# Row sums of an attention kernel taken for two head pairs at once, with a new order of work for the first eight steps

## The chip, the cores and the metric

The kernel runs on one core of a Trainium2 chip. The metric is device time in microseconds (us) of one execution of the whole kernel, lower is better. Below, the engines are called by the profile's names: PE (TensorE, matrix products; PEld is its weight loading), DVE (VectorE), ACT (ScalarE), POOL (GpSimd) and SP (SyncE, which issues DMAs).

## The reference

Attention with a soft cap on the scores, followed by a channel-mixing layer. Cut to what is computed:

```python
# B, H, S, D = 8, 12, 448, 64; float32
scores = cap * tanh(q @ k.T / sqrt(64) / cap)
attn = exp(scores - max) ; attn = attn / (sum(attn) + 1e-9)
x = (attn @ v)                      # to (8, 448, 768)
xk = mu_k * x + (1 - mu_k) * x_prev # x_prev: x shifted by one position
xr = mu_r * x + (1 - mu_r) * x_prev
k = relu(xk @ w_k)                  # 768 -> 1024
out = sigmoid(xr @ w_r) * ((k * k) @ w_v)
```

The three weights arrive as 64-bit numbers and are turned into float32 on the chip.

## The kernel before

**Pairs and steps.** The 96 heads are worked as 48 pairs of heads. Up to step 13 (`SW = 14`) the loop in `run` does one step `i` for each pair; later steps take two pairs at once and are the same in both kernels. A step is a list of words (`START_EVEN`, `START_ODD`), and `step` issues the operation of each word in the order of the list. Every engine takes its own instructions in the order in which they were issued, so the list is the program of all engines at once. A word works on a pair that hangs on the step: `S`, `L`, `tanh`, `exp`, `red` on pair `i`, `V` on pair `i - 1`, `sum_recip`, `norm`, `mix_old`, `mix_new`, `x_high`, `x_low`, `x_store`, `VL` on pair `i - 2`.

**What the words do.** The 448 keys are cut in three groups of 128 and a rest of 64; the rests of an even pair and of the odd pair behind it share one tile ("L", `p_left`).
- `S0 S1 S2` and `L` (PE, L275 and L285): scores of a key group, into one of two score tiles in PSUM. A tile can be written again once its `tanh` is done.
- `tanh`, `exp` (ACT, L291 and L301): 128 x 896 each, one `tanh` and one `exp` for each score tile.
- `V` (PE, L310): the six 64-column products with the values; `VL` (L319): the four products of the rest.
- `O` and `OL` (PE, L331 and L340): row sums, as products with a tile of ones (`self.one`, 1/32), for the pairs in `ONES` (0 to 5). The other pairs get their row sums from `red` (DVE, L356), `gather`, `recip`, `rec_store`, `rec_load`.
- `sum_recip` (DVE, L347 to L352): row sums from PSUM to reciprocals, spread over the partitions.
- `norm` (DVE, L407): values times reciprocal. `mix_old` (ACT, L417) then `mix_new` (DVE, L422) form `xk`; `mix_old` reads what `norm` wrote, `mix_new` reads what `mix_old` wrote. `x_high`, `x_low` (POOL, L127 and L137) split it for the key products.
- `K` (PE, L469): parts of `xk @ w_k`; the first falls into step 7 (`KFIRST = 28`).

**Weights beside it.** The 64-bit weights come in chunks. `weight_load` (SP, L501) loads one chunk, `more` loads extra ones in the steps named in `MORE`. `weight_abs` takes the absolute value of the high words of the loaded chunks, on DVE (L515) for the chunks in `DABS` and on ACT (L517) for the others. Each `f` then issues the next of five DVE operations (L537 to L545) on the chunks whose absolute value was issued, `weight_rest` those that are left; an `f` with no chunk does nothing. `weight_sum` (POOL, L554 and L127) and `weight_low` (DVE, L576) finish a chunk.

Of the kernel before, what the change touches and what calls it, by code (L numbers as in the profile page):

```python
# [9 lines left out]
F32 = mybir.dt.float32  # L10
F32R = mybir.dt.float32r
AF = mybir.ActivationFunctionType
ALU = mybir.AluOpType
# [3 lines left out]
B, H, S, D = 8, 12, 448, 64  # L17
# [6 lines left out]
NPAIR = B * NP  # L24
HN = DM // 2
P = 128
# [24 lines left out]
KO = (6, 4, 3, 2)  # L51
# [17 lines left out]
HALF = (slice(0, 64), slice(64, 128))  # L69
NB = 2 * S // 32  # L70
# [3 lines left out]

START_EVEN = """more weight_load gather load_qk load_v weight_store load_vl OL f sum_recip weight_low weight_rest S0 K S1 V
VL L relu tanh0 exp0 tanh1 k_store tanhL expL qk_high weight_sum f recip norm f red0 f S2 K exp1 relu mix_old
qk_low redL mix_new red1 x_high x_low k_store tanh2 K O K relu exp2 k_store f red2 weight_abs rec_store
x_store rec_load"""  # L80
START_ODD = """load_qk weight_load gather load_v sum_recip f f norm f f K S0 tanh0 exp0 mix_old relu k_store O K S1 S2 tanh2
# [8 lines left out]
LAST = """V.0 V.1 VL next gather l2 p0 recip d1 rec_store c0 rec_load l5 c1 k_store s0 c2 norm.0 norm.1 mix_old.0 mix_old.1  # L90
# [1 line left out]


def order(i):
    ops = LAST if i == NPAIR else UNIT if SW <= i <= NPAIR + 1 else START_ODD if i % 2 else START_EVEN
    if i == 8:
        ops = ops.replace("tanh2 K O K relu exp2", "K O K relu tanh2 exp2")
# [15 lines left out]
class Body:  # L113
# [189 lines left out]
    def values(self, i):  # L303

        nc, v = self.nc, self.rawv.pop(i)
        pv = self.ps_v.tile([P, 512], F32, name="pv")
        for g in range(3):
            ph = self.P32[i, g]
            for h, p in enumerate(HALF):
                nc.tensor.matmul(pv[p, 0:S], v[:, g, h, :], ph[:, h, :], start=(g == 0), stop=False)  # L310
        self.PV[i] = pv

    def values_left(self, i):


        v, ph = self.rawv.pop((i, "L")), self.P32[i, "L"]
        for p in range(2):
            for h, o in enumerate(HALF):
                self.nc.tensor.matmul(self.PV[i + p][o, 0:S], v[HALF[p], h, :], ph[HALF[p], h, :],  # L319
                                      start=False, stop=True)  # L320
# [13 lines left out]
    def ones_left(self, i):  # L334

        ph = self.P32[i, "L"]
        self.SUM[i + 1] = self.ps_k.tile([P, 512], F32, name="kps")
        for p in range(2):
            for h, o in enumerate(HALF):
                self.nc.tensor.matmul(self.SUM[i + p][o, 0:S], self.one[HALF[p]], ph[HALF[p], h, :],  # L340
                                      start=(p == 1), stop=(p == 0))

    def sum_recip(self, i):

        nc = self.nc
        t = self.up.tile([P, NB // 2], F32, name="se", bufs=1)
        nc.vector.tensor_reduce(out=t, in_=self.SUM.pop(i)[:, 0:S].rearrange("p (b k) -> p b k", k=32),  # L347
                                axis=mybir.AxisListType.X, op=ALU.add, apply_transpose=True)
        nc.vector.tensor_scalar(t, t, self.grd, None, op0=ALU.add)
# [444 lines left out]
    def step(self, i):  # L794

        even, unit = i % 2 == 0, SW <= i <= NPAIR + 1
        if unit and not even:
            return
        if self.maxima and even and i < NPAIR:
            self.row_maxima(i)  # L800
            self.row_maxima(i + 1)
        pair = dict(load_qk=i + 3, qk_high=i + 2, qk_low=i + 2, load_v=i, S=i, tanh=i, exp=i, red=i, load_vl=i, L=i)
        pair.update(dict.fromkeys("V gather recip rec_store rec_load".split(), i - 1))
        pair.update(O=i - 1, OL=i - 2)
        pair.update(dict.fromkeys("sum_recip norm mix_old mix_new x_high x_low x_store VL".split(), i - 2))
        name = dict(S="scores", V="values", VL="values_left", L="scores_left", O="ones", OL="ones_left")
        late = "gather recip rec_store rec_load red".split()
        first = "O OL sum_recip".split()
        two = "gather recip rec_store rec_load".split()
        nk = 0  # L810
        if unit:
            pair.update(VL=i - 2)
        seen = {}
        for op in order(i):
            g, j1 = (), 0
            if len(op) == 2 and op[0] in "lpdcs":
                self.tail_work(op)
                continue
            if "." in op:
                op, j1 = op[:-2], int(op[-1])  # L820
            if op[-1] in "012L" and op not in ("L", "VL", "OL"):
                op, g = op[:-1], (op[-1] if op[-1] == "L" else int(op[-1]),)
            if op in pair:
                j = pair[op] + j1
                if unit and op == "V":
                    j -= 1
                    if j < SW - 1:
                        continue
                if op in two:
                    if unit:  # L830
                        if j - 1 < NPAIR:
                            getattr(self, op + "_two")(j - 1)
                        continue
                    if j >= SW - 2:
                        continue
                if op == "load_qk" and i == 0 and Q2:
                    self.load_qk(2)
                if 0 <= j < NPAIR and op not in (late if j in ONES else first) and not (uncut(j) and op in ('qk_high', 'qk_low')):
                    getattr(self, name.get(op, op))(j, *g)
            elif op == "next":  # L840
                self.open_first()
# [216 lines left out]
```

## Time and profile before

| | |
|---|---|
| time, median of 3 runs | 896.61 us (896.44 to 896.88) |
| the profiled execution | 895.82 us, its span 894.0 us |
| PE busy | 881.2 us (99%) |
| DVE busy | 734.8 us (82%) |
| ACT busy | 623.1 us (70%) |
| POOL busy | 415.0 us (46%) |

The shares are means over the whole span. Times in the trace are counted from the start of the span. A timeline row gives the start, the time that the instructions took together, the engine, the line and the tiles; in square brackets stands how long the engine sat idle before and what ended that.

### The profile page before, as it was taken

To read this page: it belongs to the slowest core of one execution; us is meant where nothing else is said; L and a number is where in the kernel's file an instruction comes from. 1 tells how busy PE (TensorE), PEld (TensorE's weight loads), DVE (VectorE), ACT (ScalarE), POOL (GpSimd) and SP (SyncE) were. 2 spreads that over 40 slices of the span, in tenths; PEclk is the share of its full clock that TensorE was granted. 3 is DMA by queue.
4 is the path that set the end of the run, shared out by engine and by line. 5 is a ranking of instruction groups with operands and counts; after the bars stand their busy time and mean duration, and the time that the engine had idled before them with its cause. 6 is when DMAs were issued, how large, how long until landed. Compare 5 with 4: busy or idle time off the path is not lost.

```text
span 894.0 us, 14329 instructions
## 1 busy us (share of the span) xinstructions
PE 881.2 (99%) x5046; PEld 694.7 (78%) x5046; DVE 734.8 (82%) x1115; ACT 623.1 (70%) x962; POOL 415.0 (46%) x399
## 2 busy tenths in 40 slices
PE   7999999999999999999999999999999999999997
PEld 2335556767766677777676999999999999999996
DVE  5868996888987887897886789888888888888883
ACT  7898878888887787787876776655545555555451
POOL 2343354555566585676774003444345434443440
PEclk9999999999999999999999999999999999999999
DMA  7354655766656776677647963233233322332301
GB/s 261 118 167 144 207 185 163 227 193 192 193 184 193 210 224 214 201 216 243 200 148 247 330 237 95 76 110 118 79 114 110 118 87 85 119 110 83 119 28 49
DMA packets 97562, 142.97 MB, mean 160 GB/s; under 512 B 11592, under 2 KB 86984, under 8 KB 96840
## 3 DMA queue, kind: packets, MB, share of 16 engines
q1 hardware_dynamic: 89704, 129.56, 46.3%
q10 hardware_dynamic: 7776, 12.39, 3.7%
q8 instruction: 42, 0.69, 0.3%
q14 instruction: 40, 0.33, 0.1%
HBM read 94.18 MB, written 45.33 MB: 156 GB/s over the span
## 4 chain that ended last, share of the span: by engine, by line
PE 94%; ACT 3%; DVE 1%; DMA 1%; issue 0%; SPq 0%; DVEq 0%; ACTq 0%
PE kps L469 26%; PE ps2a L720 22%; PE pv L310 12%; PE ps2c L720 11%; PE s L275 11%; PE ps2b L720 5%; PE pv L319 2%; PE s L285 2%; PE kps L331 1%; ACT p L291 1%; ACT p L301 1%; DMA sq<-r 0%; DVE ro L708 0%; PE kps L340 0%; DMA w<-wk 0%
## 5 line engine op out<-in xcount | busy, mean ns | idle before, releaser
L291 ACT ACTIVATE p<-s,scl_t 128x896 f32<-128x896 f32 x144 | 139.4, 997 | 17.0 <-PE s L275 11.3
L301 ACT ACTIVATE p<-p,cap_t 128x896 f32<-128x896 f32 x144 | 145.2, 1036 | 1.9
L469 PE MATMUL kps<-xkh,wkl 128*128 128x448 f32 x384 | 143.5, 374 | 0.1
L469 PE MATMUL kps<-xkl,wkh 128*128 128x448 f32 x384 | 140.7, 366 | 0.0
L356 DVE TRANSPOSE_TENSOR_REDUCE r<-p 128x28 f32<-128x896 f32 x126 | 136.0, 1092 | 5.7 <-ACT p L301 5.4
L469 PE MATMUL kps<-xkh,wkh 128*128 128x448 f32 x384 | 140.3, 365 | 0.0
L310 PE MATMUL pv<-p,rv 128*64 128x448 f32 x576 | 115.1, 544 | 0.0
L469 PEld LDWEIGHTS kps<-xkh,wkl 128*128 128x128 f32 x384 | 72.1, 188 | 25.7 <-issue 12.3
L310 PEld LDWEIGHTS pv<-p,rv 128*64 128x64 f32 x576 | 38.6, 136 | 66.5 <-issue 57.4
L469 PEld LDWEIGHTS kps<-xkl,wkh 128*128 128x128 f32 x384 | 72.1, 188 | 8.0 <-issue 2.8
L469 PEld LDWEIGHTS kps<-xkh,wkh 128*128 128x128 f32 x384 | 72.1, 188 | 5.8
L708 DVE TENSOR_TENSOR ro<-t,ro 128x384 fp32r<-128x384 f32 x70 | 52.8, 756 | 23.2 <-ACT ro L131 23.2
L137 POOL TENSOR_TENSOR qkl<-rqk,qkh 128x832 fp32r<-128x832 f32 x34 | 67.6, 1988 | 2.7
L708 DVE TENSOR_TENSOR vo<-x,vo 128x512 fp32r<-128x512 f32 x63 | 56.3, 902 | 11.3 <-ACT vo L131 11.0
L407 DVE TENSOR_TENSOR x<-pv,r 128x448 f32<-128x448 f32 x48 | 28.1, 618 | 45.3 <-DMA r<-rec_d 43.6
L554 POOL TENSOR_TENSOR wsq<-wa,wsq 128x384 f32<-128x384 f32 x24 | 25.9, 1080 | 84.4 <-DVE wsq L545 84.4
L752 ACT ACTIVATE rs<-rs 128x384 f32<-128x384 f32 x28 | 14.7, 525 | 65.1 <-DVE rs L725 65.1
L131 ACT CAST ro<-t 128x384 fp32r<-128x384 f32 x70 | 34.3, 509 | 30.5 <-POOL t L137 30.2
L137 POOL TENSOR_TENSOR xkl<-xk,xkh 128x448 fp32r<-128x448 f32 x46 | 53.0, 1152 | 3.8
L672 DVE SCALAR_TENSOR_TENSOR t<-xc,mu_r,t 128x256 f32<-128x256 f32 (+3 forms) x120 | 53.7, 500 | 0.8
L137 POOL TENSOR_TENSOR s<-s,t 128x384 f32<-128x384 f32 x13 | 13.6, 1048 | 75.0 <-DVE ro L708 75.0
L131 ACT CAST vo<-x 128x512 fp32r<-128x512 f32 x63 | 38.9, 618 | 10.3 <-POOL x L137 6.0
(209 smaller groups left out, 2386.3 us busy)
## 6 DMA issues: line engine op xcount, KB each, us to landing
rqk<-qk SPq DMA_DIRECT2D x47, 448.0 KB
k_d<-ko ACTq DMA_DIRECT2D x54, 224.0 KB
x_d<-x SPq DMA_DIRECT2D x48, 224.5 KB
out<-cp SPq DMA_DIRECT2D x56, 192.0 KB
rv<-v SPq DMA_DIRECT2D x48, 192.0 KB
r<-rec_d SPq DMA_DIRECT2D x36, 224.0 KB
kr<-k_d SPq DMA_DIRECT2D x7, 1024.0 KB
x<-k_d SPq DMA_DIRECT2D x7, 1024.0 KB
```

The lines of the kernel that those rows point to most:

```text
L131: self.nc.scalar.copy(out, x)
L137: {"p": self.nc.gpsimd, "v": self.nc.vector}[e].tensor_sub(*a)
L275: nc.tensor.matmul(s[:, h, 0:S], qk[a][p, k], qk[b][p, 0:S], start=(n == 0), stop=(n == len(terms) - 1))
L291: self.nc.scalar.activation(p32, self.S.pop((i, g))[:, :, 0:S], AF.Tanh, scale=self.scl_t)
L301: self.nc.scalar.activation(p32, p32, AF.Exp, scale=1.0 if self.maxima else self.cap_t)
L310: nc.tensor.matmul(pv[p, 0:S], v[:, g, h, :], ph[:, h, :], start=(g == 0), stop=False)
L356: self.nc.vector.tensor_reduce(out=r1[:, :, 3 if g == "L" else g], in_=self.P32[i, g].rearrange("p h (b k) -> p (h b) k", k=32), axis=mybi ...
L407: self.nc.vector.tensor_mul(self.X[i % 2][:, 1:], self.PV[i][:, 0:S], self.R.pop(i))
L469: nc.tensor.matmul(self.kps[fc][:, 0:S], w, m[:, dc, :], start=first, stop=last)
L672: nc.vector.scalar_tensor_tensor(out=td, in0=self.XC[:, d, j0 + o + 1:j1 + o + 1], scalar=self.mu["r"][:, d:d + 1], in1=td, op0=ALU.mult, ...
L708: self.nc.vector.tensor_sub(lo, a, f(hi))
L720: self.nc.tensor.matmul(o, a[:, g], self.WS[p, g][w][:, m], start=first and part == 0 and g == 0, stop=last and part == 2 and g == KG[p] - ...
```

## The change

Pairs 0 to 5 now get their row sums for two pairs together. `ones(i)` is issued once for an even pair and covers it and the next one: sixteen products with 32 columns of ones, four to each key group, which write four strips of 32 partitions of one PSUM tile. `ones_left` is gone. `sum_recip` does the reduction from PSUM and the addition once, for the even pair, and for each pair a reciprocal, two copies of 32 partitions and the spreading.

Steps 0 to 7 have lists of their own, `ONES_EVEN` and `ONES_ODD`. In them `O` stands for pair `i - 2` and only in even steps; the values of an odd pair are started by `VL` and finished by a new word `U` one step later than before. The absolute values of chunks 0 to 8, rather than 0 and 1, are taken by DVE, and one extra chunk is loaded in step 3 instead of step 7. From step 8 on the lists are the old ones without the words for row sums.

```diff
-DABS = (0, 1)
+DABS = range(9)
-MORE = (0, 0, 1, 7, 9)
+MORE = (0, 0, 1, 3, 9)
...
+ONES_EVEN = """more weight_load gather load_qk load_v weight_store load_vl weight_low f f f S0 K S1 O S2 VL L
+sum_recip tanh0 exp0 tanh1 exp1 tanh2 exp2 f f weight_sum norm f f weight_rest weight_sum red0 K tanhL expL mix_old red1 weight_abs mix_new
+x_high x_low red2 redL K K relu k_store x_store"""
+ONES_ODD = """load_qk weight_load gather load_v weight_low f f f f f weight_sum sum_recip S0 U K tanh0 exp0 f f norm S1 K mix_old
+tanh1 exp1 mix_new x_high x_low weight_rest weight_sum red0 recip S2 V K K tanh2 exp2 relu k_store red1 weight_abs red2
+x_store rec_store weight_store more rec_load"""
...
-    ops = LAST if i == NPAIR else UNIT if SW <= i <= NPAIR + 1 else START_ODD if i % 2 else START_EVEN
+    ops = LAST if i == NPAIR else UNIT if SW <= i <= NPAIR + 1 else (ONES_ODD if i % 2 else ONES_EVEN) if i < 8 else START_ODD if i % 2 else START_EVEN
...
-        pv = self.ps_v.tile([P, 512], F32, name="pv")
+        left = i in self.PV
+        pv = self.PV[i] if left else self.ps_v.tile([P, 512], F32, name="pv")
...
     def ones(self, i):
-        if i not in self.SUM:
-            self.SUM[i] = self.ps_k.tile([P, 512], F32, name="kps")
-        for g in range(3):
-            ph = self.P32[i, g]
-            for h, p in enumerate(HALF):
-                self.nc.tensor.matmul(self.SUM[i][p, 0:S], self.one, ph[:, h, :],
-                                      start=(i % 2 == 0 and g == 0), stop=(i % 2 == 1 and g == 2))
...
+        self.SUM[i] = self.ps_k.tile([P, 512], F32, name="kps")
+        for g in (0, 1, 2, "L"):
+            for q in range(4):
+                h, p = divmod(q, 2)
+                rows = HALF[p] if g == "L" else slice(0, P)
+                ph = self.P32[i if g == "L" else i + p, g]
+                self.nc.tensor.matmul(self.SUM[i][32 * q:32 * q + 32, 0:S], self.one[rows, 0:32], ph[rows, h, :],
+                                      start=(g == 0), stop=(g == "L"))
...
-        nc.vector.reciprocal(t, t)
+        t = self.up.tile([P, NB // 2], F32, name="st", bufs=1)
+        nc.vector.reciprocal(t, self.se)
+        for h in range(2):
+            a, z = (32 * (2 * h + (i + j) % 2) for j in range(2))
+            nc.vector.tensor_copy(t[z:z + 32], t[a:a + 32])
...
-        pair.update(O=i - 1, OL=i - 2)
+        pair.update(O=i - 2, U=i - 2)
```

## Rows read from the trace of the kernel before

**Rows 1.** The windows view, stretches between first tanh of steps 2, 4, 6, 8.

```profile
core 0: us, PE busy (x) PEld busy (x) DVE busy (x) ACT busy (x) POOL busy (x), PEclk, DMA share, GB/s
...
21.15:39.13 17.98, 17.98 (x100) 5.70 (x96) 14.17 (x31) 15.95 (x20) 5.52 (x7) 1.00 0.50 152
39.13:56.25 17.12, 17.12 (x96) 5.78 (x96) 11.87 (x25) 15.47 (x19) 9.43 (x12) 1.00 0.48 151
56.25:75.57 19.32, 19.32 (x99) 8.23 (x97) 17.22 (x33) 15.60 (x20) 5.68 (x9) 1.00 0.27 85
```

**Rows 2.** The chain that ended last: start, us, what (PE, steps 2 to 5).

```profile
26.88 2.41 PE kps L331 x12
29.29 0.95 PE s L275 x4
...
36.83 0.91 PE kps L340 x8
```

**Rows 3.** The timeline of ACT, steps 0 to 7.

```profile
5.90 1.01 ACT L291 ACTIVATE p<-s,scl_t 128x896 f32<-128x896 f32 x1
...
28.92 0.62 ACT L417 ACTIVATE pv<-x,om_k 128x448 f32<-128x448 f32 x1
...
38.69 0.54 ACT L517 ACTIVATE wsq<-w 128x384 f32<-128x384 f32 x1
...
49.49 0.99 ACT L291 ACTIVATE p<-s,scl_t 128x896 f32<-128x896 f32 x1
50.51 1.04 ACT L301 ACTIVATE p<-p,cap_t 128x896 f32<-128x896 f32 x1
51.46 0.62 ACT L417 ACTIVATE pv<-x,om_k 128x448 f32<-128x448 f32 x1
52.02 1.88 ACT L291 ACTIVATE p<-s,scl_t 128x896 f32<-128x896 f32 x2
...
70.75 0.64 ACT L417 ACTIVATE pv<-x,om_k 128x448 f32<-128x448 f32 x1 [1.69 <-DVE x L407]
```

**Rows 4.** The timeline of DVE, steps 0 to 7.

```profile
6.12 0.37 DVE L194 COPY lz<-grd 32x28 f32<-32x28 f32 x2
...
9.84 0.36 DVE L515 TENSOR_SCALAR wsq<-w 128x384 uint32<-128x384 uint32 x1 [1.85 <-DMA w<-wk]
10.11 0.35 DVE L537 TENSOR_SCALAR wt<-wsq 128x384 f32<-128x384 f32 x1
...
12.48 0.36 DVE L537 TENSOR_SCALAR wt<-wsq 128x384 f32<-128x384 f32 x1
...
15.79 1.19 DVE L537 TENSOR_SCALAR wt<-wsq 128x384 f32<-128x384 f32 x1
...
22.49 0.24 DVE L350 RECIPROCAL se<-se 128x14 f32<-128x14 f32 x1
...
29.57 0.68 DVE L422 SCALAR_TENSOR_TENSOR xk<-x,mu_k,pv 128x448 f32<-128x448 f32 x1 [2.39 <-ACT pv L417]
...
31.39 0.65 DVE L352 STREAM_TRANSPOSE r<-se 128x448 f32<-128x448 f32 x1
32.03 0.36 DVE L537 TENSOR_SCALAR wt<-wsq 128x384 f32<-128x384 f32 x1
...
32.70 0.62 DVE L407 TENSOR_TENSOR x<-pv,r 128x448 f32<-128x448 f32 x1
...
72.08 0.55 DVE L576 TENSOR_TENSOR wkl<-wsq,wkh 128x384 fp32r<-128x384 f32 x1
...
75.22 2.10 DVE L356 TRANSPOSE_TENSOR_REDUCE r<-p 128x28 f32<-128x896 f32 x2
```

**Rows 5.** The timeline of PE: products after the start, in step 1, step 8.

```profile
3.99 3.36 PE L275 MATMUL s<-rqk 64*128 64x448 f32 x8 [3.99 <-DMA rqk<-qk]
...
15.06 1.77 PE L275 MATMUL s<-rqk 64*128 64x448 f32 x8
...
76.35 2.48 PE L310 MATMUL pv<-p,rv 128*64 128x448 f32 x12
```

More of the change, by code (lines that the diff above doesn't have):

```diff
@@ L70 @@
 NB = 2 * S // 32
-START_EVEN = """more weight_load gather load_qk load_v weight_store load_vl OL f sum_recip weight_low weight_rest S0 K S1 V
+ONES_EVEN = """more weight_load load_qk load_v weight_store load_vl weight_low f f f S0 K S1 O S2 VL L
+sum_recip tanh0 exp0 tanh1 exp1 tanh2 exp2 f f weight_sum norm f f weight_rest weight_sum red0 K tanhL expL mix_old red1 weight_abs mix_new
[3 more added lines that the diff above has]
+x_store rec_store weight_store more rec_load"""
+START_EVEN = """more weight_load gather load_qk load_v weight_store load_vl f weight_low weight_rest S0 K S1 V
 VL L relu tanh0 exp0 tanh1 k_store tanhL expL qk_high weight_sum f recip norm f red0 f S2 K exp1 relu mix_old
-qk_low redL mix_new red1 x_high x_low k_store tanh2 K O K relu exp2 k_store f red2 weight_abs rec_store
+qk_low redL mix_new red1 x_high x_low k_store tanh2 K K relu exp2 k_store f red2 weight_abs rec_store
 x_store rec_load"""
-START_ODD = """load_qk weight_load gather load_v sum_recip f f norm f f K S0 tanh0 exp0 mix_old relu k_store O K S1 S2 tanh2
+START_ODD = """load_qk weight_load gather load_v f f norm f f K S0 tanh0 exp0 mix_old relu k_store K S1 S2 tanh2
 tanh1 relu exp1 k_store exp2 V f weight_low red0 recip mix_new weight_rest weight_sum x_high qk_high qk_low
@@ L309, in values @@
             for h, p in enumerate(HALF):
-                nc.tensor.matmul(pv[p, 0:S], v[:, g, h, :], ph[:, h, :], start=(g == 0), stop=False)
+                nc.tensor.matmul(pv[p, 0:S], v[:, g, h, :], ph[:, h, :],
+                                 start=(g == 0 and not left), stop=(g == 2 and left))
         self.PV[i] = pv
@@ L316, in values_left @@
         v, ph = self.rawv.pop((i, "L")), self.P32[i, "L"]
+        first = i + 1 not in self.PV
+        if first:
+            self.PV[i + 1] = self.ps_v.tile([P, 512], F32, name="pv")
         for p in range(2):
+            new = first and p == 1
             for h, o in enumerate(HALF):
-                self.nc.tensor.matmul(self.PV[i + p][o, 0:S], v[HALF[p], h, :], ph[HALF[p], h, :],
-                                      start=False, stop=True)
+                self.nc.tensor.matmul(self.PV[i + p][o, 0:S], v[HALF[p], h, :], ph[HALF[p], h, :], start=new, stop=not new)
@@ L324, in ones @@
     def ones(self, i):
-        if i not in self.SUM:
-            self.SUM[i] = self.ps_k.tile([P, 512], F32, name="kps")
-        for g in range(3):
-            ph = self.P32[i, g]
-            for h, p in enumerate(HALF):
-                self.nc.tensor.matmul(self.SUM[i][p, 0:S], self.one, ph[:, h, :],
-                                      start=(i % 2 == 0 and g == 0), stop=(i % 2 == 1 and g == 2))
[L334 to L341, printed above, removed]
+        self.SUM[i] = self.ps_k.tile([P, 512], F32, name="kps")
@@ L347, in sum_recip @@
-        nc.vector.tensor_reduce(out=t, in_=self.SUM.pop(i)[:, 0:S].rearrange("p (b k) -> p b k", k=32),
-                                axis=mybir.AxisListType.X, op=ALU.add, apply_transpose=True)
-        nc.vector.tensor_scalar(t, t, self.grd, None, op0=ALU.add)
-        nc.vector.reciprocal(t, t)
+        if i % 2 == 0:
+            self.se = self.up.tile([P, NB // 2], F32, name="se", bufs=1)
+            nc.vector.tensor_reduce(out=self.se, in_=self.SUM.pop(i)[:, 0:S].rearrange("p (b k) -> p b k", k=32),
+                                    axis=mybir.AxisListType.X, op=ALU.add, apply_transpose=True)
+            nc.vector.tensor_scalar(self.se, self.se, self.grd, None, op0=ALU.add)
@@ L803, in step @@
         pair.update(dict.fromkeys("V gather recip rec_store rec_load".split(), i - 1))
-        pair.update(O=i - 1, OL=i - 2)
+        pair.update(O=i - 2, U=i - 2)
         pair.update(dict.fromkeys("sum_recip norm mix_old mix_new x_high x_low x_store VL".split(), i - 2))
-        name = dict(S="scores", V="values", VL="values_left", L="scores_left", O="ones", OL="ones_left")
+        name = dict(S="scores", V="values", U="values", VL="values_left", L="scores_left", O="ones")
         late = "gather recip rec_store rec_load red".split()
-        first = "O OL sum_recip".split()
+        first = "O sum_recip".split()
         two = "gather recip rec_store rec_load".split()
@@ L820, in step @@
                 op, j1 = op[:-2], int(op[-1])
-            if op[-1] in "012L" and op not in ("L", "VL", "OL"):
+            if op[-1] in "012L" and op not in ("L", "VL"):
                 op, g = op[:-1], (op[-1] if op[-1] == "L" else int(op[-1]),)
```

3 lines of the change are left out of this document (1 added, 2 removed).

## The prediction

> **What bounds the kernel now.** I read the windows first, cut at the first `tanh` of steps 2, 4, 6 and 8 [rows 1]. The reader is to see that PE is busy for the whole of each stretch (17.98 of 17.98 us, 17.12 of 17.12, 19.32 of 19.32), with ACT close behind (15.95, 15.47, 15.60) and DVE third. The chain of waits then says what PE does there: it goes from one PE group to the next without a gap, and the row sums are a visible part of it. `O` takes 2.41 us for a pair, `OL` 0.91 us for two [rows 2], so two steps hold 2 x 2.41 + 0.91 = 5.73 us of row sums. A cut in them is worth something only as long as PE stays the engine that the others wait for. So I read the timelines of ACT and DVE, to see how much room they have. ACT's own pace: `tanh` 1.02 (49.49 to 50.51), `exp` 0.95 (50.51 to 51.46), `mix_old` 0.56 (51.46 to 52.02), so one score tile costs 1.97 us [rows 3]. Two steps hold seven tiles and two `mix_old`: 13.79 + 1.12 = 14.9 us. Once in this stage ACT waited for DVE: `mix_old` at 70.75 stood 1.69 us idle until `norm` (L407) was done [rows 3]. That wait is the one to follow through the new lists.
>
> **The row sums on PE.** Old: 12 records (two for each product) in 2.41 us, two column halves side by side [rows 2]. New: twelve full-height products, 24 records, and the four of the rest. If four strips run side by side, 24 records take what 12 took, 2.41, and the rest 0.91: 3.32 us, a saving of 2.41 us in each two steps, 7.2 us for the three. If only two strips run side by side, the first part is 4.82 and nothing is saved. No row shows four full-height strips at once; the nearest, `OL`, runs its 8 records (64 x 64) in 0.91, against 2.41 for 12, so 0.11 us a record against 0.20, four at a time [rows 2]. I take 3.32.
>
> The Trainium skill, TensorE: Matmul & The Clock Gate, section Measured speedup vs the span model, gives 2.38 times for three strips of 32 columns, not 3 times. An estimate from that page makes the first part 2.41 x 3 / 2.38 = 3.0 us, 0.6 more in each two steps, and my sum 905.4 instead of 903.5; no row here can decide between them.
>
> **The other moved costs.** On DVE, three reductions and additions go. Per pair two copies of 32 partitions come, 0.37 together by the nearest row (L194, two copies of 32 x 28), and seven absolute values at 0.36 [rows 4]; on ACT seven absolute values at 0.54 go [rows 3]. Of the DMAs only one chunk's load moves on SP, from step 7 to step 3; it stands at the end of the step with `x_store` ahead of it, and its data are not wanted before the end of step 4. I cost it at nothing: the wait for `norm`, below, is the cover, and without it one load is about what DVE waited between two chunks, under 2 us [rows 4]. `U` moves the values of odd pairs, at equal cost.
>
> **The new order.** This is where I choose. In an odd step the new list puts `mix_old` on ACT behind one `tanh` and one `exp`, ahead of the other two. It needs `norm`. On DVE, `norm` stands behind `mix_new` of the even step, which itself needs that step's `mix_old`, now the last thing that ACT does in the even step. Between them DVE has: `weight_low`, five `f`, reciprocal, two copies, spreading, two more `f`. By the chunk counts, in steps 3 and 5 all seven `f` are real work (chunks 4 and 5, 7 and 8). From the start of the even `mix_old`:
> `mix_new` starts after 0.65 (28.92 to 29.57) [rows 3, 4]; it takes 0.68, `weight_low` 0.55, five `f` 2.37 (10.11 to 12.48), reciprocal 0.24, copies 0.37, spreading 0.64 (31.39 to 32.03), two `f` 0.67 (32.03 to 32.70), `norm` 0.62 [rows 4]. Sum 6.79.
> To this comes what POOL does to the `f`: right behind `mix_new` it runs `x_high` and `x_low`, then the chunk's sum. Five `f` in a row took 2.37 once and 3.31 when L537 and L539 stretched to three times their time (12.48 to 15.79) [rows 4]. Bounds 0 and 1.4 (both `f` runs hit), I take 0.9, nearer to the second since POOL has work there each time: 7.7 us.
> ACT meanwhile has `mix_old`, `tanh`, `exp`: 0.56 + 1.02 + 0.95 = 2.53. So it waits 5.2 us in steps 3 and 5. Behind the waiting `mix_old` are two `tanh` and two `exp`, and behind those the next score tiles on PE, which can't be written until a `tanh` frees a tile: PE has S1, S2 and `V` to do, then stands still some 3.5 us.
> In step 7 the two `f` before `norm` are empty (one chunk only), but `red2` and `redL` of pair 6 come ahead, 2.10 [rows 4]: 6.79 - 0.67 + 2.10 + 0.9 = 9.1; ACT has 2.53 and one absolute value 0.54, so it waits 6.05.
> In the even steps `O` must wait for the last `exp`; then 3.32 + 0.95 for S2 = 4.27 against the 3.94 of two tiles on ACT, with a hand-over 0.43 late, three times 1.29. `norm` is in time there: in step 2 the third chunk's data come at about 12.05 (an estimate: 9.84 plus one operation of 0.36 and a wait of 1.85 as before it), three chunks take 2.37 + 3.31 + 3.31, and with one absolute value before and one after, three `weight_low`, three `f`, sum, reciprocal and spreading (2.2), two `f` and `norm` it ends at 28.3, ACT arrives at 28.0.
>
> **The sum.** ACT starts at 5.90 [rows 3] and runs seven tiles of steps 0 and 1 with nothing between: 19.69. Then 21 tiles 41.37, six `mix_old` 3.36, two absolute values 1.08, waits 5.2 + 5.2 + 6.05 = 16.45, late tiles 1.29. The last `exp` of step 7 ends at 83.2. `V` of pair 7 needs it; before, that `V` started at 76.35 [rows 5]. From step 8 on the lists are the old ones, so I let the shift stand to the end: +6.9 us. The profiled execution took 895.82 us, 0.79 under the median, so 902.7 for it and **903.5** against the median of 896.61. Own range: without POOL's part, with smaller hand-overs and neighbouring DVE operations overlapping a little (-3.8) 899.7; with 1.4 three times, later tiles, and the third chunk late by up to 1.2 (+3.2) 906.7. A measurement of this kernel tells about 0.2%, 1.8 us, from no change.
>
> **Rivals.**
> 1. Faster: DVE reaches `norm` while ACT still has work, so the wait vanishes and PE's saving counts: 896.6 - 7.2 = 889.4. For it: in the old steps 3 and 5 `mix_old` did not wait. Against it: there only `mix_new`, sum, reciprocal, spreading and two `f` lay between (29.57 to 33.32, 3.75 us [rows 4]), and the even `mix_old` came before the last tile, not after it. It decides when the waits are below 16.45 - 6.9 = 9.6 us, that is the DVE run under about 5.5 us in place of 7.7; the undisturbed rows already make 6.8. Chance 0.13.
> 2. The waits come out about 2 us shorter each and eat just the saving: 896.6. Chance 0.07.
> 3. Four strips don't run side by side: `O` 5.73, S2 late by 2.8 instead of 0.4, three times 2.4 = +7.2 on top: 910.7. Chance 0.08.
> 4. PE's clock falls in the gaps that the waits tear. The granted clock reads 1.00 in all stretches [rows 1], full speed (2.4 GHz), with no gap to test it. But the first 8 records, after 3.99 us without work, took 3.36 us where 8 alike took 1.77 in step 1 [rows 5]: half the speed. If the 5 us behind each gap ran so, the `O` in it would be some 2.5 us later, +7.5 in all: 911. Chance 0.07.
>
> For the fourth, the Trainium skill, TensorE: Matmul & The Clock Gate, section HAM oscillation, says that waits between bursts of products bring the clock back to half. By that rule 911, by the column of the granted clock alone 903.5.
>
> **The numbers.** Mine 0.65. Slower: 0.65 + 0.08 + 0.07 = 0.80; same 0.07; faster 0.13. The range from 898 to 911 leaves out the first two rivals, 0.20. Mine alone: 899.7 to 906.7.
>
> **What would show it.** In the profile after: `mix_old` (L417's successor) on ACT idle 4 to 7 us behind DVE's `norm` in steps 3, 5 and 7, PE gaps of about 3 us ahead of the first scores of steps 4, 6 and 8, 32 records of row sums in about 3.3 us, `V` of pair 7 near 83, and the same shift at the end as there. I am wrong if ACT runs without those waits, or if the shift at step 8 is made good later.

## The result and the profile after

The changed kernel takes 908.34 us (median of six runs, 907.25 to 911.0) where the kernel before takes 896.53 beside it (six runs, 894.68 to 897.06): a ratio of 1.0138, 95% interval 1.0121 to 1.0155. It is 11.8 us slower. The forecast was 6.9 us slower: the side is right, but the time lies above what my own case allowed (899.7 to 906.7); it is inside the range only because I drew that up to 911 for the third and fourth rivals.

I read the same views again, cut at the same places. First the windows of the changed kernel: three stretches of two steps each, between the first `tanh` of steps 2, 4, 6 and 8 (`V` of pair 7 starts with the last cut, at 90.03); below them two short stretches around one gap on PE. Columns as in [rows 1].

```profile
core 0: us, PE busy (x) PEld busy (x) DVE busy (x) ACT busy (x) POOL busy (x), PEclk, DMA share, GB/s
20.84:42.69 21.85, 16.86 (x100) 5.18 (x96) 19.94 (x39) 14.92 (x16) 9.12 (x11) 0.91 0.41 120
42.69:66.13 23.44, 18.44 (x100) 5.35 (x96) 18.60 (x35) 15.33 (x18) 9.08 (x11) 0.86 0.43 142
66.13:90.05 23.92, 22.40 (x121) 8.58 (x119) 19.00 (x36) 15.81 (x20) 7.91 (x12) 0.93 0.23 71
36.00:39.80 3.80, 0.01 (x2) 0.01 (x2) 2.93 (x8) 1.59 (x3) 0.70 (x3) 0.84 0.20 63
39.80:44.00 4.20, 4.09 (x12) 1.20 (x16) 3.80 (x5) 4.13 (x5) 3.54 (x4) 0.50 0.98 288
```

In [rows 1] PE was busy for the whole of each stretch. Now it stands idle for 4.99 and 5.00 us of the first two (21.85 - 16.86, 23.44 - 18.44), and DVE has become the fullest engine there. It is busy for 18.6 to 19.9 us in the three stretches, against 11.9 to 17.2 before; in the third PE is still ahead of it (22.40). The granted clock (the column PEclk) has changed too: it was 1.00 in all three stretches and is now 0.86 to 0.93, and 0.50 in the 4.2 us behind the gap.

The timeline of ACT in the changed kernel: the `mix_old` of step 2, which did not wait, and then each wait of steps 3 to 7.

```profile
29.78 0.62 ACT L425 ACTIVATE pv<-x,om_k 128x448 f32<-128x448 f32 x1
...
38.18 0.64 ACT L425 ACTIVATE pv<-x,om_k 128x448 f32<-128x448 f32 x1 [5.78 <-DVE x L415]
...
48.82 1.01 ACT L297 ACTIVATE p<-s,scl_t 128x896 f32<-128x896 f32 x1 [2.09 <-PE s L281]
...
61.18 0.64 ACT L425 ACTIVATE pv<-x,om_k 128x448 f32<-128x448 f32 x1 [5.78 <-DVE x L415]
...
72.26 1.01 ACT L297 ACTIVATE p<-s,scl_t 128x896 f32<-128x896 f32 x1 [2.10 <-PE s L281]
...
85.09 0.64 ACT L425 ACTIVATE pv<-x,om_k 128x448 f32<-128x448 f32 x1 [5.79 <-DVE x L415]
```

Two kinds of wait alternate. The `mix_old` of steps 3, 5 and 7 (L425) waits 5.78, 5.78 and 5.79 us for `norm`; the single wait of this kind before was 1.69 [rows 3]. And one `tanh` of S2 in steps 4 and 6 (L297) waits 2.1 us for scores. Two smaller ones of the second kind, 1.03 and 0.93, stand in step 2. Together 17.35 us for `norm` and 6.15 for scores.

The timeline of DVE in the changed kernel, from the even step's `mix_new` (L430) to the odd step's `norm` (L415):

```profile
30.43 0.68 DVE L430 SCALAR_TENSOR_TENSOR xk<-x,mu_k,pv 128x448 f32<-128x448 f32 x1 [0.55 <-ACT pv L425]
31.02 0.55 DVE L584 TENSOR_TENSOR wkl<-wsq,wkh 128x384 fp32r<-128x384 f32 x1
31.49 0.72 DVE L545 TENSOR_SCALAR wt<-wsq 128x384 f32<-128x384 f32 x1
32.25 1.19 DVE L547 TENSOR_SCALAR wa<-wt 128x384 uint32<-128x384 uint32 x1
...
34.93 0.23 DVE L355 RECIPROCAL st<-se 128x14 f32<-128x14 f32 x1
35.20 1.09 DVE L358 COPY st<-st 32x14 f32<-32x14 f32 x2
36.33 0.65 DVE L360 STREAM_TRANSPOSE r<-st 128x448 f32<-128x448 f32 x1
...
37.52 0.62 DVE L415 TENSOR_TENSOR x<-pv,r 128x448 f32<-128x448 f32 x1
```

DVE does not rest in this run; it does the weights first and the small chain that leads to `norm` behind them. The first two `f` took 0.72 and 1.19 us here, and 0.32 and 0.36 when they ran again 5 us later. The timeline of POOL shows what stood beside them:

```profile
31.19 0.81 POOL L133 TENSOR_SCALAR xkh<-xk 128x448 fp32r<-128x448 f32 x1 [1.53 <-DVE xk L430]
32.08 1.14 POOL L143 TENSOR_TENSOR xkl<-xk,xkh 128x448 fp32r<-128x448 f32 x1
35.09 0.99 POOL L562 TENSOR_TENSOR wsq<-wa,wsq 128x384 f32<-128x384 f32 x1 [1.88 <-DVE wsq L553]
```

`x_high` and `x_low` lie beside the two long `f`, the chunk's sum (L562) beside the two copies.

The timeline of PE in the changed kernel: row sums of step 2, then what follows the gap of step 3, then `V` of pair 7.

```profile
21.47 2.46 PE L343 MATMUL kps<-p,one 128*32 128x448 f32 x24
23.86 0.96 PE L343 MATMUL kps<-p_left,one 64*32 64x448 f32 x8
...
39.79 3.84 PE L281 MATMUL s<-rqk 64*128 64x448 f32 x8 [4.89 <-ACT p L297]
43.56 3.37 PE L343 MATMUL kps<-p,one 128*32 128x448 f32 x24
...
90.03 2.48 PE L317 MATMUL pv<-p,rv 128*64 128x448 f32 x12
```

24 records of 32 columns took 2.46 us, what 12 records of 64 columns took before (2.48 in the timeline, which is the view shown here; 2.41 in the chain of [rows 2]). After 4.89 us without work, eight records of scores took 3.84 where [rows 5] has 1.77, and the row sums behind them 3.37. `V` of pair 7 starts 13.7 us later than in [rows 5].

### The profile page after: what moved, and what is told of

Its sections match the earlier page's. It is cut to its first block, busy times and chain, and to the rows that moved or that the text cites. A ratio compares the mean times of both kernels' runs of the same rounds, so it can differ in the third digit from the quotient of the medians.

```text
span 906.9 us, 14314 instructions
## 1 busy us (share of the span) xinstructions
PE 880.8 (97%) x5046; PEld 693.7 (76%) x5046; DVE 744.4 (82%) x1128; ACT 620.3 (68%) x955; POOL 414.6 (46%) x399
## 4 chain that ended last, share of the span: by engine, by line
PE 89%; DVE 5%; ACT 4%; DMA 1%; issue 0%; SPq 0%; DVEq 0%; ACTq 0%
PE kps L477 26%; PE ps2a L728 22%; PE ps2c L728 11%; PE pv L317 10%; PE s L281 10%; PE ps2b L728 5%; PE pv L331 2%; ACT p L297 2%; PE s L291 2%; ACT p L307 1%; PE kps L343 1%; DVE r L364 1%; DVE st L358 0%; ACT pv L425 0%; DVE wa L547 0%
## 5 line engine op out<-in xcount | busy, mean ns | idle before, releaser
L297 ACT ACTIVATE p<-s,scl_t 128x896 f32<-128x896 f32 x144 | 139.6, 996 | 23.3 <-PE s L281 18.7
L562 POOL TENSOR_TENSOR wsq<-wa,wsq 128x384 f32<-128x384 f32 x24 | 25.6, 1066 | 86.6 <-DVE wsq L553 84.6
L281 PE MATMUL s<-rqk 64*128 64x448 f32 x168 | 46.9, 656 | 18.4 <-ACT p L297 13.2
L415 DVE TENSOR_TENSOR x<-pv,r 128x448 f32<-128x448 f32 x48 | 28.2, 618 | 44.1 <-DMA r<-rec_d 43.9
L425 ACT ACTIVATE pv<-x,om_k 128x448 f32<-128x448 f32 x48 | 30.1, 629 | 28.5 <-DVE x L415 28.5
```

What stands on the lines that cost most here:

```text
L281: nc.tensor.matmul(s[:, h, 0:S], qk[a][p, k], qk[b][p, 0:S], start=(n == 0), stop=(n == len(terms) - 1))
L297: self.nc.scalar.activation(p32, self.S.pop((i, g))[:, :, 0:S], AF.Tanh, scale=self.scl_t)
L425: self.nc.scalar.mul(self.xold[i], self.X[i % 2][:, 0:S], self.om["k"][:, hp:hp + 1])
```

## The experiments

All edits are against the changed kernel. The column "shift" is where `V` of pair 7 starts, less 76.35 [rows 5]; the ratio is to the kernel before on the same chip, whose median was 894.9 to 896.5. Differences of the shift under some 1.6 us are not safe: PE has the same work in steps 0 and 1 of the changed kernel, e1, e3 and e12, but the `tanh` of S2 in step 2 starts at 25.82 in the changed kernel's profile and at 24.19 to 24.63 in those three, since the granted clock of step 1 was lower in the first (last section). The changed kernel's even list has no `gather`; the one printed with the change shows the word, but it would do nothing in those steps.

| kernel | median us | ratio (95%) | waits for `norm` before `V` of pair 7 | shift us |
|---|---|---|---|---|
| changed | 908.34 | 1.0138 (1.0121 to 1.0155) | 5.78, 5.78, 5.79 | +13.7 |
| e1_norm_first | 904.39 | 1.0112 (1.0095 to 1.0129) | 1.58, 3.00, 1.55, 2.99, 3.40 | +3.5 |
| e2_fill_gap | 905.3 | 1.0113 (1.0097 to 1.013) | 5.80, 5.78, 5.80 | +9.9 |
| e3_split_late | 906.27 | 1.0118 (1.0102 to 1.0135) | 5.16, 4.67, 5.88 | +12.6 |
| e4_abs_act | 909.36 | 1.0164 (1.0147 to 1.0181) | 4.87, 4.86, 5.80 | +14.4 |
| e5_old_lists | 907.41 | 1.0132 (1.0115 to 1.0149) | 1.12 (others: see text) | +11.9 |
| e6_norm_first_act | 900.65 | 1.0065 (1.0048 to 1.0082) | 2.98, 0.56, 2.38 | +1.1 |
| e7_own_lists | 899.41 | 1.0046 (1.0029 to 1.0063) | 4.79, 1.27 | +5.4 |
| e8_own_lists_dve | 903.9 | 1.0103 (1.0086 to 1.012) | 0.76, 0.42, 4.80, 1.33, 5.38, 1.48 | +5.9 |
| e9_spread | 891.69 | 0.9952 (0.9935 to 0.9968) | 1.65 | -3.9 |
| e10_spread_dve | 892.37 | 0.9953 (0.9937 to 0.997) | 1.35, 0.19, 1.67 | -3.4 |
| e11_spread_old_sums | 898.5 | 1.0035 (1.0019 to 1.0051) | 1.88 | +3.0 |
| e12_mix_late | 904.65 | 1.0112 (1.0095 to 1.0128) | 1.87, 2.75, 2.41, 2.28, 3.07 | +3.9 |

**Is it the order on DVE?** e1 puts the chain to `norm` ahead of the weight work in the odd list, and nothing else.

```diff
-load_qk weight_load gather load_v weight_low f f f f f weight_sum sum_recip S0 U K tanh0 exp0 f f norm S1 K mix_old
-tanh1 exp1 mix_new x_high x_low weight_rest weight_sum red0 recip S2 V ...
+load_qk weight_load gather load_v sum_recip S0 U K tanh0 exp0 norm S1 K mix_old
+tanh1 exp1 mix_new x_high x_low weight_low f f f f f weight_sum f f weight_rest weight_sum red0 recip S2 V ...
```

> In the odd steps below 8, sum_recip and norm stand ahead of weight_low and the seven f on DVE; the rest is as in the changed kernel. Theory (ACT waits in mix_old for what DVE has to do ahead of norm): the run from the even mix_old to the odd norm falls from 8.4 to about 3.3 us, the waits in steps 3 and 5 from 5.78 to about 1 us, in step 7 from 5.79 to about 3; the weight work then delays the even norm by some 2 us, so about 897 to 900 us. Rival (DVE is simply full, the order doesn't matter): the wait comes back whole in the even steps, and the time stays within 2 us of 908.3.

The waits of the odd steps fell from 5.8 to between 1.55 and 3.40 us, and `V` of pair 7 came 10.1 us earlier. But the even steps, which had no wait, now wait 3.00 and 2.99, and the rest comes in step 8. There `norm` of pair 6 stands on DVE behind `recip` of pair 7. That needs the row sums of pair 7, whose reductions DVE reached only at 82.32 to 84.37, behind the moved `f`, and whose gathering by DMA it then waited for. ACT waited 4.14 us for `norm`, and PE 4.19 before its first chain of step 8, as these rows of e1 show (ACT, DVE, PE):

```profile
68.46 0.64 ACT L425 ACTIVATE pv<-x,om_k 128x448 f32<-128x448 f32 x1 [2.99 <-DVE x L415]
74.95 0.64 ACT L425 ACTIVATE pv<-x,om_k 128x448 f32<-128x448 f32 x1 [3.40 <-DVE x L415]
...
91.25 0.64 ACT L425 ACTIVATE pv<-x,om_k 128x448 f32<-128x448 f32 x1 [4.14 <-DVE x L415]
```

```profile
89.49 0.61 DVE L377 TENSOR_REDUCE sr<-sq 32x28 f32<-32x448 f32 x1 [2.55 <-DMA sq<-r]
```

```profile
92.41 0.74 PE L477 MATMUL kps<-xkh,wkl 128*128 128x448 f32 x1 [4.19 <-ACT ko L487]
92.95 0.57 PE L477 MATMUL kps<-xkl,wkh 128*128 128x448 f32 x1
```

Of the 10.1 us, 6.2 are left at that chain (92.41 against 98.57), and in the whole time 3.9 by the medians or 2.3 by the ratios, whose intervals overlap; I had expected 897 to 900. So the wait does follow the order, but the order alone gives back only a part of the loss: in these lists DVE's work comes due at another place.

**e12** leaves DVE's order alone and makes ACT ask later: the odd `mix_old` moves behind `exp2`.

```diff
-... f f norm S1 K mix_old
-tanh1 exp1 mix_new x_high x_low weight_rest weight_sum red0 recip S2 V K K tanh2 exp2 relu ...
+... f f norm S1 K
+tanh1 exp1 S2 V K K tanh2 exp2 mix_old mix_new x_high x_low weight_rest weight_sum red0 recip relu ...
```

> The changed kernel with mix_old of the odd steps behind the last exp on ACT, and mix_new behind it on DVE; DVE's run up to norm is the same. Theory (the 5.8 us are lost because tanh1, exp1, tanh2 and exp2 queue behind the waiting mix_old): the run from even mix_old to norm stays 8 to 8.5 us, but ACT has 6.5 us of work until then, so the waits fall to about 1.9 us, the gap in PE and the halved clock vanish, V of pair 7 starts 8 to 12 us earlier than 90.0, the time falls by 6 us or more, to 902 or less. Rival (it is DVE's sum that sets the pace in these steps): the waits move to the even norm and the time stays within 2 us of 908.

The same picture from the other side: `V` of pair 7 came 9.8 us earlier, waits of 1.9 to 3.1 us stand in even and odd steps alike, PE stood idle 3.66 us in step 8, and the ratio is that of e1. The odd waits are near the 1.9 that I had expected, but the even steps wait too, as the rival said, and the time is not the 902 or less of the theory.

**The clock behind the gap.** e2 fills PE's gaps in steps 3 and 5 with products into a tile that nothing reads.

```diff
-... recip S2 V K K tanh2 ...
+... recip S2 V fill K K tanh2 ...
+            if op == "fill":
+                if i in (3, 5):
+                    t = self.ps_k.tile([P, 512], F32, name="kps")
+                    for n in range(11):
+                        self.nc.tensor.matmul(t[HALF[n % 2], 0:S], self.one, self.P32[i - 1, n % 3][:, n % 2, :], start=True, stop=True)
+                continue
```

> Eleven products with the ones tile (22 records, about 4.4 us at full clock), whose result nobody reads, stand behind V in steps 3 and 5, in PE's gap. Theory (the gap halves PE's clock, and the scores and row sums behind it come late for that): the granted clock behind the gaps stays at 1.0, the two products of scores and the 24 records behind the gap take 1.77 and 2.46 again instead of 3.84 and 3.4 to 3.8, ACT's waits of 2.09 and 2.10 before S2's tanh in steps 4 and 6 fall to 0.5 to 0.9, the time falls by about 3 us to 905. Rival (the 32-column products are slow by themselves or wait for something else): no change, 908.

ACT and then PE in e2, around the first of the two gaps:

```profile
38.32 0.64 ACT L425 ACTIVATE pv<-x,om_k 128x448 f32<-128x448 f32 x1 [5.80 <-DVE x L415]
...
47.20 1.01 ACT L297 ACTIVATE p<-s,scl_t 128x896 f32<-128x896 f32 x1 [0.34 <-PE s L281]
```

```profile
34.86 4.67 PE L828 MATMUL kps<-p,one 128*64 128x448 f32 x22
...
42.86 2.46 PE L343 MATMUL kps<-p,one 128*32 128x448 f32 x24
```

The wait for `norm` is the same (5.80), the wait for scores falls from 2.09 to 0.34 and that of step 6 from 2.10 to nothing, the row sums take 2.46 again, and `V` of pair 7 comes 3.8 us earlier. In the 4.2 us from 39.80 the granted clock is 1.00 in e2, where it was 0.50. So this part of the loss is the clock, not the lists. In the whole time work that does nothing gained 3.0 us by the medians, 2.2 by the ratios, whose intervals overlap; the trace is the surer evidence.

**POOL beside the `f`.** e3 moves `x_high` and `x_low` of pairs 0, 2 and 4 to the following odd step, behind its last chunk's sum, with a second buffer for `xk`.

```diff
-        self.xk = self.up.tile([P, S], F32, name="xk", bufs=1)
+        self.xk = self.up.tile([P, S], F32, name="xk", bufs=2)
...
-x_high x_low red2 redL K K relu ...
+xa red2 redL K K relu ...
...
-tanh1 exp1 mix_new x_high x_low weight_rest weight_sum red0 recip S2 V ...
+tanh1 exp1 mix_new weight_rest weight_sum xe x_high x_low red0 recip S2 V ...
...
+            if op == "xa":
+                self.xke = self.xk if i > 1 else None
+                continue
+            if op == "xe":
+                if i > 2:
+                    new, self.xk = self.xk, self.xke
+                    self.x_high(i - 3)
+                    self.x_low(i - 3)
+                    self.xk = new
+                continue
```

> x_high and x_low of the pairs 0, 2 and 4 are issued on POOL one step later, behind the last weight sum of the odd step, with a second buffer for xk. Theory (these two POOL operations stretch the f of the odd steps, 0.72 and 1.19 instead of 0.39 and 0.40): the run from mix_old to norm falls from 8.4 to about 7.2, each of the three waits by 1.1 to 1.5 us, the time by 3 to 5 us to about 904. Rival (the stretching comes from other work, or the run is as long without it): the waits stay at 5.78 and the time at 908.

DVE in e3, the same two `f` and the copies:

```profile
30.46 0.35 DVE L545 TENSOR_SCALAR wt<-wsq 128x384 f32<-128x384 f32 x1
30.84 0.36 DVE L547 TENSOR_SCALAR wa<-wt 128x384 uint32<-128x384 uint32 x1
...
32.96 1.10 DVE L358 COPY st<-st 32x14 f32<-32x14 f32 x2
```

The `f` fall from 0.72 and 1.19 to 0.35 and 0.36; the copies, whose neighbour (the chunk's sum) was not moved, stay at 1.10. From `mix_new` to `norm` the run is 5.90 us instead of 7.09 (29.40 to 35.30; 30.43 to 37.52). The waits fall by 0.6 and 1.1, not at all in step 7; of that, longer waits for scores (2.13, 2.66 and, in step 8, 2.80 for 2.09, 2.10 and 1.22) took a part again. `V` of pair 7 comes 1.1 us earlier, which is less than step 2's own earlier start (24.19 for 25.82); and the time, 906.27, missed the 904 that I had expected, with an interval that overlaps the changed kernel's. The stretching is shown; that the kernel gains without it is not.

**The absolute values alone.** e4 gives them back to ACT.

```diff
-DABS = range(9)
+DABS = (0, 1)
```

> The absolute values of chunks 2 to 8 go back to ACT, nothing else changes. Theory (the wait comes from the order of the odd steps; the absolute values lie outside that run): waits of 5.3 to 5.8 us remain, ACT gets about 0.5 us more on its path in steps 1 and 3, the time is 908 to 910. Rival (the absolute values overload DVE): each wait shrinks by 1 us or more and the time falls by 3 us or more.

The waits fell by 0.9 in steps 3 and 5 and the time did not: it rose, if anything. From one `mix_old` to the next it is 8.42 us, as in the changed kernel (28.62 to 37.04 here, 29.78 to 38.18 there). In the changed kernel's lists ACT waits anyway, and its own absolute values only fill a part of the wait. With `norm` ahead of the weight work the same edit, together with the extra chunk back in step 7, is worth some 4 us (e6 against e1: 3.7 by the medians, 4.2 by the ratios):

```diff
-DABS = range(9)
-MORE = (0, 0, 1, 3, 9)
+DABS = (0, 1)
+MORE = (0, 0, 1, 7, 9)
```

> The run with sum_recip and norm first, and the absolute values of chunks 2 to 8 on ACT and the extra chunk in step 7 again, as in the kernel before. Theory (with the order mended, what is left is DVE's sum of work): DVE loses 7 absolute values and one chunk until step 7, the waits in the even steps (3.0 us) fall to about 1, V of pair 7 starts near 77 in place of 79.9, the time is 898 to 901. Rival (the sum of DVE's work doesn't matter): the same as the run with norm first, 904.

**The row sums alone.** e5 keeps the lists of before and changes only the row sums: `O` for two pairs behind S1 of the even step, `sum_recip` of the even pair behind `expL`; `DABS` and `MORE` as before.

```diff
+ONES_EVEN = """more weight_load gather load_qk load_v weight_store load_vl f weight_low weight_rest S0 K S1 O V
+VL L relu tanh0 exp0 tanh1 k_store tanhL expL weight_sum sum_recip f recip norm f red0 f S2 K exp1 relu mix_old
...
+ONES_ODD = """load_qk weight_load gather load_v sum_recip f f norm f f K S0 tanh0 exp0 mix_old relu k_store K S1 S2 tanh2
...
```

> Only the row sums are changed: the first eight steps have the old lists, with O (for two pairs, 32 columns) in the even step behind S1 and sum_recip of the even pair behind expL; absolute values and chunk loads as in the kernel before. Theory (in these lists ACT, not only PE, sets the pace: L stands behind O, V and VL, 7.4 us of PE work, and ACT has three operations until then): in each even step ACT waits some 4 us for L in place of 1.9, in the odd steps it waits for nothing, so 895 to 902 us, no gain from 7.2 us less PE work. Rival (PE's work alone counts): 7 us less, 888.

It is as slow as the changed kernel, in another way. ACT waits 5.04, 5.13 and 5.14 us for the scores of the rest, L, since `O` of two pairs, `V` and `VL` all stand ahead of L on PE; and in the odd steps PE runs dry and slows:

```profile
56.57 1.87 PE L282 MATMUL s<-rqk 64*128 64x448 f32 x4 [2.43 <-ACT p L298]
58.99 1.86 PE L282 MATMUL s<-rqk 64*128 64x448 f32 x4 [0.55 <-ACT p L298]
60.78 3.54 PE L318 MATMUL pv<-p,rv 128*64 128x448 f32 x12
```

I had expected 895 to 902. In these lists PE's saved time is worth nothing: it falls where PE waits for ACT, and ACT waits for PE elsewhere.

**Lists of my own.** If the theory holds, lists in which `norm` comes early, the weight work is spread, and ACT keeps its absolute values should win. e7 is the first of them: `norm` first in odd steps, the even `mix_old` between `tanhL` and `expL`, and five `f` ahead of the even `sum_recip`. e8 is e7 with the changed kernel's `DABS` and `MORE`.

```diff
+ONES_EVEN = """more weight_load load_qk load_v weight_store load_vl weight_low f f f f f S0 K S1 O S2 VL L
+tanh0 exp0 tanh1 exp1 red0 sum_recip norm tanh2 exp2 weight_sum weight_rest weight_sum red1 K tanhL mix_old expL mix_new
+x_high x_low red2 redL weight_abs K K relu k_store x_store"""
+ONES_ODD = """load_qk weight_load gather load_v sum_recip S0 U K tanh0 exp0 norm S1 K mix_old
+tanh1 exp1 mix_new x_high x_low red0 recip weight_low f f red1 S2 V K K tanh2 exp2 f f f red2 weight_sum weight_rest weight_sum relu k_store weight_abs
+x_store rec_store weight_store more rec_load"""
```

> Lists of my own on the changed row sums: norm first in the odd steps, mix_old of the even pair between tanhL and expL, five f ahead of sum_recip in the even steps while DVE waits for O, the reductions red1 and red2 of step 7 ahead of most of the f; absolute values and chunk loads as in the kernel before. Theory (mix_old waits and DVE's sum are the whole loss): no wait of ACT above 1 us in steps 2 to 6, two steps take about 16.3 us on ACT (14.9 and three absolute values), V of pair 7 starts at 71 to 74, the time is 2 to 5 us under the kernel before, 890 to 893. Rival (the row sums for two pairs at once delay S2 or norm by themselves): not under 895.

> The same lists with the absolute values of chunks 0 to 8 on DVE and the extra chunk in step 3, as in the changed kernel. Theory (DVE is the fuller engine): 1 to 4 us slower than the run with the absolute values on ACT. Rival (ACT is the fuller one): 1 to 2 us faster than it.

e7 missed its forecast of 890 to 893: one wait of 4.79 us is left, in step 4, where the chunks pile up ahead of `norm`, and it brings a PE gap of 4.85 with it. e8 is 4.5 us slower than e7 on the same chip, with waits of 4.80 and 5.38: with DVE the fuller engine, the seven absolute values and the earlier chunk, changed together, do cost.

e9 takes the pile apart: two `f` behind `norm` in the even step, two behind `norm` and eight behind `mix_new` in the odd one, and a chunk more in step 2. Absolute values and chunk loads are those of the kernel before.

```diff
+ONES_EVEN = """more weight_load load_qk load_v weight_store load_vl S0 K S1 O S2 VL L
+tanh0 exp0 tanh1 exp1 red0 sum_recip norm tanh2 exp2 red1 f f weight_sum K tanhL mix_old expL mix_new
+x_high x_low red2 redL weight_abs K K relu k_store x_store"""
+ONES_ODD = """load_qk weight_load gather load_v sum_recip S0 U K tanh0 exp0 norm f f weight_sum S1 K mix_old
+tanh1 exp1 mix_new x_high x_low red0 recip weight_low f f f red1 S2 V K K tanh2 exp2 f f weight_sum f f f weight_sum red2 relu k_store weight_abs
+x_store rec_store weight_store more rec_load"""
+    if i == 1:
+        ops = ops.replace("S1 K mix_old", "S1 V K mix_old").replace("S2 V K K", "S2 K K").replace("red2", "weight_rest weight_sum")
+    if i == 2:
+        ops = ops.replace("S0 K S1 O", "weight_low f f f f f weight_sum S0 K S1 O")
```

> My own lists again, with the weight work spread so that no more than two f stand between mix_new and the next norm on DVE: two f behind the even norm, two behind the odd norm, eight behind the odd mix_new; in step 1 V stands ahead of S2, so that PE has less of a gap at the start. Theory (what is left of the loss in the first own lists is one wait of 4.79 us for norm in step 4 and the halved clock behind it): no wait for norm above 1.5 us, PE at full clock throughout, V of pair 7 at 73 to 76, the time 891 to 895, at or a little under the kernel before. Rival (DVE's sum is still too much, the wait only moves): a wait of 3 us or more in another place, 897 to 900.

> The same with the absolute values of chunks 4, 5 and 7 on DVE too. Theory (ACT is the fuller engine once the waits are gone): 0.5 to 1.5 us faster than the run with them on ACT. Rival (DVE is): 0.5 to 2 us slower.

The windows of e9 from 14 to 80 us (columns as above), and the one wait for `norm` in its ACT timeline:

```profile
14.00:80.00 66.00, 64.41 (x377) 23.14 (x376) 59.72 (x114) 59.65 (x69) 27.66 (x34) 1.00 0.50 158
```

```profile
64.89 0.64 ACT L429 ACTIVATE pv<-x,om_k 128x448 f32<-128x448 f32 x1 [1.65 <-DVE x L419]
```

PE is busy 64.41 of 66 us at a clock of 1.00, where the changed kernel has 55.17 at 0.87 in the same stretch. The time is 0.9952 of that of the kernel before: of all the runs only this one and e10 beat both kernels. e10 gives three of the absolute values (chunks 4, 5 and 7) to DVE again and is the same (0.9953): it told its two theories not apart, but in these lists DVE has room for those three.

e11 is e9 with the old row sums, 64 columns and a tile for each pair, in the same places; `sum_recip` reduces each pair by itself again.

```diff
+        for p in range(2):
+            self.SUM[i + p] = self.ps_k.tile([P, 512], F32, name="kps")
+            for g in range(3):
+                for h, o in enumerate(HALF):
+                    self.nc.tensor.matmul(self.SUM[i + p][o, 0:S], self.one, self.P32[i + p, g][:, h, :], start=(g == 0), stop=False)
...
```

> The spread lists with the row sums of the kernel before: at the place of O stand the 64-column products of both pairs, one PSUM tile for each, and sum_recip reduces each pair by itself. Theory (the 32-column products are worth their 2.41 us in lists where PE is followed by a waiting ACT): O takes about 5.7 us in place of 3.3, ACT waits 2 to 2.5 us for S2 in each even step, the time is 5 to 8 us over the run with the spread lists, 897 to 900. Rival (ACT sets the pace and PE has room): at most 1.5 us over it.

PE and ACT in e11:

```profile
20.11 4.73 PE L345 MATMUL kps<-p,one 128*64 128x448 f32 x24
```

```profile
45.15 1.01 ACT L301 ACTIVATE p<-s,scl_t 128x896 f32<-128x896 f32 x1 [2.17 <-PE s L285]
```

4.73 against 2.46 us, and ACT waits 2.17 to 2.18 for S2 three times. The shift is 6.8 us worse than in e9 (79.32 against 72.50), the time 7.4 by the ratios ((1.0035 - 0.9952) x 895.5). DVE's share in `sum_recip` changes with them, but ACT's only wait for `norm` is 1.88 us, for 1.65 in e9. So the 32-column sums are worth what the prediction put on them (7.2), in lists that let ACT and DVE keep up.

## Why the prediction was right in sign and short in size

- **The row sums.** Forecast 2.41 + 0.91 = 3.32 us, measured 2.46 + 0.96. The third rival (strips not side by side) is out. So is the estimate of 3.0 us for the first part from the Trainium skill, TensorE: Matmul & The Clock Gate, section Measured speedup vs the span model: here 24 records in four strips took the time of 12 in two (no run has one strip alone). The saving of 7.2 us is real (e11), and it was lost.
- **The waits for `norm`.** Forecast 5.2, 5.2 and 6.05, measured 5.78, 5.78 and 5.79: a sum of 17.35 for 16.45. The gaps on PE that I had put at some 3 us were 4.89, 4.89 and 1.52. That the waits come from the order is shown by e1 and e12, which take most of each odd wait away. The first rival needed a run from `mix_old` to `norm` of under 5.5 us, the second one some 2 us shorter than 7.7; it was 8.4 (29.78 to 38.18).
- **The term of POOL was too small.** I took 0.9 us for it, at most 1.4, and for the `f` alone. Measured, the run was 8.40 for 6.79 undisturbed: 1.6. The five `f` took 3.44 (31.49 to 34.93) for 2.37, so 1.1, inside my bounds. The copies took 1.13 to the next operation (35.20 to 36.33), 0.76 more than the 0.37 at which I had priced them whatever stood beside them; the other rows came out 0.2 shorter. (In the row run from 12.48 that I took as the stretched one, it was L539 that took three times its time; L537 did so in the run from 15.79.)
- **What a tensor_scalar meets there.** The stretched operations run beside POOL's and not without it (e3: 1.19 to 0.36). The Trainium skill, SBUF — State Buffer, section Who interferes with whom, says that DVE's copies and tensor-scalar operations in their two-port modes and GpSimd lock each other out of a shared pair of ports, an instruction at a time; the trace agrees for the `f`, and for the copies in this place no run took the neighbour away.
- **The term that failed: late tiles.** The step "S2 late by 0.43, three times 1.29" is the one that was mis-sized: ACT's waits for scores came to 6.15 us. Its cause was the fourth rival, which I had set apart with a chance of 0.07 instead of seeing that my own case, by its PE gaps, brings it along. The granted clock is 0.50, the lower of its two levels (1.2 GHz), behind a gap of 4.89 us, and with the gap filled S2 is on time: e2 takes 3.85 us of these waits away. The 1.96 us of step 2 have another source, the slow products of step 1 shown at the end: they stay in e2 (2.04), but e1, e3 and e12, with the same work on PE until then, have only 0.50 to 0.51. So 1.5 us of the 4.9 above my forecast came and went with the execution, and how many of the six runs had them is not known. The Trainium skill, TensorE: Matmul & The Clock Gate, section HAM oscillation, says that waits between bursts throttle the next burst. By that rule the sum was 911; here the trace agrees (0.50 behind both gaps of 4.89 us), and the median of 908.34 lies between that and 903.5. It is not the whole 7.5 us, since the third gap was short: in step 7 PE stood idle 1.52 us ahead of S and kept its full clock.
- **The sum.** ACT's forecast end of step 7 was 83.2. With the measured waits in place of mine it is 83.2 + 0.9 + 4.9 = 89.0; measured 89.7. The other 0.7 is my price of `exp`: 0.95 is its time until the next operation starts (39.77 to 40.72), but ahead of a wait it runs its whole 1.04 (31.35 to 32.39), and there are seven waits and the last `exp`: 8 x 0.09 = 0.7.
- **What I had costed at nothing.** The load of the extra chunk in step 3: DVE waited for no chunk between 12.13 and the end of step 7. `norm` of step 2 was in time, as worked out (`mix_old` at 29.78 did not wait).
- **The shift to the end.** At the first chain of step 8 it is 13.76 us (98.57 against 84.81), in the spans 12.9 (906.9 and 894.0), in the medians 11.8. That nothing is made good later holds but for 0.9 us: 0.4 before 504 us (13.34 there), and 0.4 behind it whose place stays open. The rest, down to 11.8, lies in the two executions that the traces are of: 908.89 is 0.55 over its median and 895.82 is 0.71 under it.
- **What I had not seen: DVE's sum.** My argument was about the order of DVE's queue. e1 and e12 undo the order's effect and still keep waits of 2 to 3 us in even steps and 3 to 4 in step 8, and e8 against e7 (4.5 us) and e6 against e1 (4 us) show the load itself: in these lists the seven absolute values and the earlier extra chunk push it past what the steps can hold. The two were changed together there, so their shares stay open. By the ratios the order alone (e1) gave back 2.3 of 12.4 us (not clear of noise), the lighter load with it (e6 against e1) 4.2, and the spread lists (e9 against e6) 10.1, the largest part. How much of the load the spread lists could still carry is not known: e10 put three of the seven absolute values back without loss, and all seven were not tried.

## What to carry to other kernels

A saving on the engine that sets the pace is worth what the next two engines can follow: work out their load in the same stretch, and the run of in-order work ahead of each hand-over, before the saving is counted. When a forecast contains a gap of several microseconds on PE, count the slower clock behind it as part of the same case. And when work is moved off an engine that waits, the engine that it lands on can pay: here seven operations of 0.36 us and an earlier chunk cost some 4 us, while three of the seven cost nothing that could be measured once the lists were spread.

## What the runs showed of the hardware beside that

- The clock can fall with small gaps too. In steps 0 and 1 the first row sums are gone, and PE waits 0.95 to 0.98 us between short groups of scores, four records at a time. The group at 12.87 still took 1.02; then one took 1.86 and the twelve records of `V` 3.20 instead of 2.48, at a granted clock of 0.67 from 14.84 to 19.77. It does not fall each time: e12 has the same work and the same gaps of 0.95, and there the group took 1.02 and `V` 2.48, at a granted clock of 1.00. e1 and e3 are like e12, e2 is like the changed kernel. In the PE timelines of the changed kernel and of e12:

```profile
12.87 1.02 PE L281 MATMUL s<-rqk 64*128 64x448 f32 x4 [0.95 <-ACT p_left L297]
14.84 1.86 PE L281 MATMUL s<-rqk 64*128 64x448 f32 x4 [0.95 <-ACT p L297]
16.63 3.20 PE L317 MATMUL pv<-p,rv 128*64 128x448 f32 x12
```

```profile
13.25 1.02 PE L281 MATMUL s<-rqk 64*128 64x448 f32 x4 [0.95 <-ACT p_left L297]
15.22 1.02 PE L281 MATMUL s<-rqk 64*128 64x448 f32 x4 [0.95 <-ACT p L297]
16.17 2.48 PE L317 MATMUL pv<-p,rv 128*64 128x448 f32 x12
```

- Two copies of 32 x 14 took 1.09 us beside POOL's sum of a chunk, and 0.34 with POOL idle (at 26.12 in the changed kernel). In e3, `weight_low`, an operation with two inputs, took 1.35 (at 38.94) beside such a sum (38.84 to 39.88). In the changed kernel it took 1.35 too beside one (42.32, the sum from 42.21), and 0.55 at 31.02, where POOL's operation began 0.17 us behind it and took 0.81 for 0.57.
- Idle products can pay: 22 records that nobody reads, in each of two gaps, brought `V` of pair 7 3.8 us forward (e2).
